# The last block's output products by seven block products, with weight sums formed on GpSimd and kept in DRAM

## The chip, the cores and the metric

One core of a Trainium2 chip runs the whole program. The metric is the device time of one execution in microseconds, as the median of the runs. The core has a matrix engine (PE, with weight loads shown apart as PEld), a vector engine (DVE), an activation engine (ACT), GpSimd (POOL), and a queue engine (SP) that issues the DMAs.

## The reference

Chunked attention with 8 memory keys gives `x` of 3072 tokens by 512. After it comes a two-layer network with a leaky bend; its second product is what the change touches:

```python
def _moe_ref(x, w_in, w_out, alpha):        # x 3072x512, w_in 512x2048, w_out 2048x512
    h = x @ w_in
    g = np.maximum(h, 0.0) + alpha * np.minimum(h, 0.0)
    return (g @ w_out).astype(np.float32)
```

## The kernel before

**Tiling.** The 3072 tokens are 8 half-blocks of `BT` = 384. The first two run plainly, each with 16 slices `f` of 128 hidden columns. The other six form three big blocks of 768 tokens, `big(0)`, `big(1)`, `big(2)`. Every fp32 operand is held as a high and a low part, and every product is three matmuls: high by low, low by high, high by high.

**A big block.** The up product (`x @ w_in`) is done for a pair of slices at a time, `pair(i)`, i = 0 to 7, in Strassen's way: seven block products for eight, 42 matmuls of 384 columns (L1194). DVE adds their PSUM results up (`add_in`, L1215), ACT and DVE make the bend (`bent`, L1084 and L1087), and `rooms` splits a bent slice into its two parts: a cast on ACT (L1100) and a subtraction on DVE (L1104), into one of four rooms used in turn. A pair leaves four bent tiles: `c11` and `c21` belong to the first 384 tokens (slices 2i and 2i+1), `c12` and `c22` to the second 384. The first two are split at once; the other two are kept (`kept_at`).

**The down product.** `chunk(which, f, tt)` multiplies one slice with 128 tokens against all 512 output columns: three matmuls of 512 columns (L1126), accumulated in a PSUM bank over all 16 slices. `whole(0, f)` for the slices of pair i-1 stands behind the products of pair i. After the last pair come the rest of `which` 0, and then `which` 1 with the slices in the order `later[s]`, each split by `take` just ahead of its use. `leave` copies the sums out of PSUM on ACT (L1259) and sends them.

**Weights.** They do not stay in SBUF. The up weights of a pair (`far_a`, `far_b`, with their Strassen sums) and the output weights of a pair (`far_o`) lie in DRAM and are loaded into slots 9 to 15, each with a queue of its own (`queues`, `load`), a slot's next load standing behind the last use of what it holds. The Strassen sums of the up weights are made by `sum_far(i, gate)`: on POOL two sums of the high and low part (L914), four sums and differences (L917) and two low parts (L925), on ACT two casts (L922), then two writes to DRAM by SP (L928). Pairs 0 to 4 are summed early; pairs 5, 6 and 7 late (`LATE_AT`), inside the big blocks.

**Order.** All work is first listed as steps with an engine, a cost and what they read and write. `Plan.send` sorts them by these costs into one fixed order for each engine, in which `rest` (a due time counted back from the end, with the constant `BIG`) decides between steps that could start. A write to DRAM is assumed to land 3.1 us after its issue (`LAND`), plus the step's `more`. On the chip each engine follows its order and waits where something is late.

**Attention inside the big blocks.** Blocks 0 and 1 still carry the attention of later units: `meet` puts value products and new scores on PE, and `weights` and `turn` put one POOL product (L415) and 21 transposes on DVE (L436) for each unit. `forms` subtracts and splits the next block's inputs (L989 on POOL; L971 on ACT; L975 on POOL and DVE). Block 2 carries no attention.

Of the kernel before, what the change touches and what calls it, by code (L numbers as in the profile page):

```python
# [70 lines left out]

HOP, LAND, FOLLOW = 0.07, 3.1, 0.1
# [15 lines left out]
PAIR, BIG = 4.7, 438.4  # L88
# [16 lines left out]
LATE_AT = {(0, 0): 5, (0, 5): 6, (1, 2): 7}  # L105
# [3 lines left out]
FIRST_SLOW = 28  # L109

# [84 lines left out]
def body(ctx: ExitStack, tc: tile.TileContext, qvw, kw, whole, heads, w_in, w_out, alpha, out):  # L195
# [53 lines left out]
    nc.scalar.activation(out=warm, in_=warm, func=AF.Exp)  # L249

# [599 lines left out]
    def store(blk, o_ps):  # L850
        def copy(tt, at_, o):
            if blk == 1:
                o["t"] = kept[tt]
                nc.vector.tensor_tensor(out=o["t"], in0=o_ps[tt], in1=o["t"], op=ALU.add)
            else:
                o["t"] = at_[0].tile([P, DM], F32, name="o_t", tag=at_[1])
                nc.scalar.copy(out=o["t"], in_=o_ps[tt])

        def send(tt, o):
            r = blk * BT + tt * P  # L860
            nc.sync.dma_start(out=out[r:r + P, :], in_=o["t"])

        for tt in range(NTT):
            at_ = (None, None, [("tmp", tt)]) if blk == 1 else leave_at(0)
            o = {}
            place = PLACE[blk, NF - 1] + 1
            step(DVE if blk == 1 else ACT, 0.68 if blk == 1 else 0.59, partial(copy, tt, at_, o), reads=okeys(blk),
                 writes=at_[2], rest=rest(place))
            step(SP, 0.75, partial(send, tt, o), reads=at_[2])
# [4 lines left out]
    far_r = {i: far.tile([P, 4 * HALF], F32, name=f"far_r{i}", tag=f"r{i}") for i in range(FIRST_LATE, NFP)}  # L874
    far_o = [far.tile([P, 2, 2, DM], F32, name=f"far_o{i}", tag=f"o{i}") for i in range(NFP)]
# [19 lines left out]
    def sum_far(i, gate):  # L895
        late = i >= FIRST_LATE
# [12 lines left out]
        def full(n):  # L909
            w = t[n] if late else ws[2 * i + n, 0].bitcast(F32)  # L910
# [18 lines left out]

        whole = [[("rs", n, 0), ("rs", n, 1)] + ([("f", n, 1)] if n or late else []) for n in range(2)]  # L930
# [4 lines left out]
        def raw_sum(n):  # L935
            step(POOL, 1.3, partial(full, n),
                 reads=gate + ([("f", n, 0)] if late else [("w", 0, 2 * i + n, 0), ("w", 0, 2 * i + n, 1)]), writes=whole[n])
# [4 lines left out]
        def form(n, to, key):  # L942
# [3 lines left out]
                 more=3.0 if late else 0.0)  # L946
            step(SP, 0.7, partial(put, n, to), reads=[("f", n, 0), ("f", n, 1)], writes=[key], more=FETCH / 2 if late else 0.0)

        a, b = far_a[i], far_b[i]
        raw_sum(0)  # L950
        raw_sum(1)
        add((1, 1), (1, 0), (1, 1), ALU.add)
# [64 lines left out]
    for b in range(NBIG):  # L1017
        for i in pairs_of[b]:
# [3 lines left out]
            queues[13 + i % 3].append(("o", b, 0, i))  # L1022
# [3 lines left out]
        for j, f in zip(order[NSTAY:], ([9, 10] if b == NBIG - 1 else []) + [11, 12] + stay):  # L1026
            queues[f].append(("o", b, 1, j))
    for f, q in queues.items():
        for x in q:
            home[x] = f  # L1030

    def load(f):
# [3 lines left out]
        x = queues[f].pop(0)  # L1036
        into = x[0] == "i"
# [22 lines left out]
    fresh = []  # L1060

    def big(s):
        ups, downs = UP[s % 2], UP[1 - s % 2]
        half = NPLAIN + 2 * s
        o = [{}, {}]
        pairs = pairs_of[s]
        turns = [list(BEFORE) if s == 0 else [], later[s]]
# [111 lines left out]

        def pair(i):  # L1180
# [47 lines left out]
            sk = bent(h, "c11", lambda: h[0], ("tmp", 0), f0)  # L1228
            rooms(g[0, f0], "c11", f0, lambda: h["c11"], sk)
# [8 lines left out]
            sk = bent(h, "c21", lambda: h[2], ("tmp", 2), f1)  # L1238
            rooms(g[0, f1], "c21", f1, lambda: h["c21"], sk)
# [3 lines left out]
            if i:  # L1243
                for f in (2 * i - 2, 2 * i - 1):
                    whole(0, f)
            if i:
                used(0, i - 1)
# [7 lines left out]
        def leave(which, tts, end=False):  # L1255
# [5 lines left out]
            def send(tt, x):  # L1261
                r = (half + which) * BT + tt * P
                nc.sync.dma_start(out=out[r:r + P, :], in_=x["t"])

            def send_half(tt, x, i):
                r, cols = (half + which) * BT + tt * P, slice(i * DM // 2, (i + 1) * DM // 2)
                (nc.scalar, nc.sync)[i].dma_start(out=out[r:r + P, cols], in_=x["t"][:, cols])

            for tt in tts:
                at_, x = leave_at(1 if s == 0 else 2), {}  # L1270
                step(ACT, 0.59, partial(copy, tt, at_, x), reads=[(downs, ups)[which][tt][2]], writes=at_[2],
                     rest=BIG - clock[0])
                if end and tt == NTT - 1:
                    for i in range(2):
                        step((ACT, SP)[i], 0.4, partial(send_half, tt, x, i), reads=at_[2])
                else:
                    step(SP, 0.75, partial(send, tt, x), reads=at_[2])
# [51 lines left out]
        for i in pairs:  # L1329
            if (s, i) in LATE_AT:  # L1330
                sum_far(LATE_AT[s, i], [("pair", s, i - 1)] if i else [("gate", len(ORDER) - 1)])
            think()
# [5 lines left out]
        last = s == NBIG - 1  # L1338
        if (s, NFP) in LATE_AT:
            sum_far(LATE_AT[s, NFP], [("pair", s, pairs[-1])])  # L1340
        rest_of = later[s]
# [8 lines left out]
        for n, f in enumerate(rest_of[:NF - NEND] if last else rest_of):  # L1350
            if n < 2:
                continue
            think()
            take(f)
# [5 lines left out]
        if not last:  # L1360
            leave(1, range(NTT))
            return
        for f in rest_of[NF - NEND:]:
            take(f)
        for tt in range(NTT):
            for f in rest_of[NF - NEND:]:
                chunk(1, f, tt)
            leave(1, [tt], end=True)
# [133 lines left out]
```

## Time and profile before

| | |
|---|---|
| three runs | 579.97, 580.73, 580.74 us, median 580.73 |
| span of the profiled execution | 578.6 us (first to last instruction) |
| PE, PEld busy | 569.9 us (98%), 505.1 us (87%) |
| DVE, ACT, POOL busy | 447.4 us (77%), 301.9 us (52%), 167.8 us (29%) |
| DMA | 154.68 MB, 267 GB/s over the span |
| big blocks 0, 1, 2 begin at about | 174, 316, 451 us |

The profiled execution has its own time: its span is 2.1 us under the median of the runs, which counts what lies around the span too. A PE row's busy time is modelled, since matmuls overlap; how fast matmuls follow each other is read from the chain of work, where each piece stands with its length and count.

### The profile page before, as it was taken

Reading aid. Unit: us, or ns where it says so; the run is one execution under the profiler, and the core shown is the slowest. Engines: PE = TensorE matmul, PEld = TensorE weight load, DVE = VectorE, ACT = ScalarE, POOL = GpSimd, SP = SyncE. Lnnn points to the kernel's source line nnn. Section 1 sums busy time; section 2 is a strip of 40 time slices with the busy share of each in tenths; the row PEclk is TensorE's granted clock in tenths of the full one; section 3 lists DMA queues with packets and bytes.
Section 4 is the critical chain, followed back from the end, with each engine's and each line's share of the span. In section 5 each row is a group of like instructions: output and inputs, shape, how many; then the busy total and the mean of one; then the engine's idle time right before and its main releaser. Section 6 shows DMA issues by size and latency. Waiting matters only on the chain.

```text
span 578.6 us, 11932 instructions
## 1 busy us (share of the span) xinstructions
PE 569.9 (98%) x4467; PEld 505.1 (87%) x4467; DVE 447.4 (77%) x995; ACT 301.9 (52%) x780; POOL 167.8 (29%) x190
## 2 busy tenths in 40 slices
PE   7999999999999999999999999999999999999997
PEld 4898989898989998999888998899888999999885
DVE  7989999888978999998989899876575566466420
ACT  3888888655665644536655453335434433223421
POOL 5640000046799935007416233003014300000000
PEclk9999999999999999999999999999999999999999
DMA  8999990386977779888797987784665867774601
GB/s 317 395 418 416 412 374 1 137 314 212 374 277 251 259 294 387 289 290 327 255 337 261 320 302 272 293 294 160 239 221 208 301 219 271 261 258 165 258 1 55
DMA packets 42090, 154.68 MB, mean 267 GB/s; under 512 B 4784, under 2 KB 10160, under 8 KB 34480
## 3 DMA queue, kind: packets, MB, share of 16 engines
q1 hardware_dynamic: 41888, 153.79, 72.5%
q8 instruction: 35, 0.57, 0.4%
q14 instruction: 23, 0.19, 0.1%
q10 hardware_dynamic: 144, 0.13, 0.1%
HBM read 122.97 MB, written 30.93 MB: 266 GB/s over the span
## 4 chain that ended last, share of the span: by engine, by line
PE 95%; DMA 2%; DVE 2%; ACT 0%; issue 0%; DVEq 0%
PE b_ps L1126 34%; PE b_ps L1194 28%; PE h_ps L774 12%; PE o_ps L804 12%; PE b_ps L1163 3%; PE a_ps L459 3%; PE s_ps L360 2%; DMA early<-heads 2%; PE a_ps L619 1%; PE o_ps L606 1%; DVE u L1215 1%; DVE pt L436 0%; PE s_ps L335 0%; DVE den L581 0%; DVE gl L1104 0%
## 5 line engine op out<-in xcount | busy, mean ns | idle before, releaser
L1194 PE MATMUL b_ps<-xf,wa 128*128 128x384 f32 x924 | 166.6, 336 | 0.3 <-ACT plain L533 0.2
L1194 PEld LDWEIGHTS b_ps<-xf,wa 128*128 128x128 f32 x924 | 160.9, 188 | 3.8 <-DVE u L1215 1.1
L1215 DVE TENSOR_TENSOR u<-b_ps,u 128x384 f32<-128x384 f32 x154 | 78.3, 551 | 47.3 <-PE b_ps L1194 41.8
L436 DVE STREAM_TRANSPOSE pt<-e 32x192 f32<-32x192 f32 (+1 forms) x336 | 100.0, 301 | 9.3 <-PE a_ps L459 2.1
L1084 ACT ACTIVATE g<-u 128x384 f32<-128x384 f32 x88 | 45.9, 525 | 77.8 <-DVE u L1215 69.2
L1126 PE MATMUL b_ps<-wo,xh 128*128 128x512 f32 x276 | 85.4, 391 | 0.0
L1126 PE MATMUL b_ps<-wo,gh 128*128 128x512 f32 x276 | 85.4, 391 | 0.0
L415 POOL TENSOR_TENSOR e<-e,den 128x384 f32<-128x384 f32 x24 | 20.9, 885 | 174.2 <-DVE den L409 77.4
L774 PE MATMUL h_ps<-xh,w 128*128 128x384 f32 x256 | 65.4, 336 | 0.0
L1126 PEld LDWEIGHTS b_ps<-wo,gh 128*128 128x128 f32 x276 | 51.8, 188 | 10.4
L1126 PEld LDWEIGHTS b_ps<-wo,xh 128*128 128x128 f32 x276 | 51.8, 188 | 10.4
L1126 PE MATMUL b_ps<-wo,gl 128*128 128x512 f32 x138 | 54.2, 393 | 0.0
L1126 PE MATMUL b_ps<-wo,xl 128*128 128x512 f32 x138 | 53.9, 391 | 0.0
L804 PE MATMUL o_ps<-w,xh 128*128 128x512 f32 x168 | 52.6, 394 | 0.0
L774 PEld LDWEIGHTS h_ps<-xh,w 128*128 128x128 f32 x256 | 46.4, 188 | 0.9
L394 ACT ACTIVATE e<-s_ps,mx 128x64 f32<-128x64 f32 x144 | 43.0, 327 | 4.1 <-DVE mx L386 4.1
L774 PE MATMUL h_ps<-xl,w 128*128 128x384 f32 x128 | 44.0, 344 | 0.0
L989 POOL TENSOR_TENSOR plain<-plain 128x384 f32<-128x384 f32 x24 | 26.3, 1116 | 44.2 <-ACT plain L533 43.0
L804 PEld LDWEIGHTS o_ps<-w,xh 128*128 128x128 f32 x168 | 31.5, 188 | 6.2
L804 PE MATMUL o_ps<-w,xl 128*128 128x512 f32 x84 | 33.0, 393 | 0.0
L394 ACT ACTIVATION_READ_ACCUMULATOR e<-s_ps,mx 128x1 f32 x144 | 31.7, 220 | 0.0
L1126 PEld LDWEIGHTS b_ps<-wo,gl 128*128 128x128 f32 x138 | 25.9, 188 | 5.5
(120 smaller groups left out, 889.2 us busy)
## 6 DMA issues: line engine op xcount, KB each, us to landing
wo<-far_o SPq DMA_DIRECT2D x37, 1024.0 KB, 6.3
wa<-far_a SPq DMA_DIRECT2D x22, 1024.0 KB, 7.3
wa<-far_b SPq DMA_DIRECT2D x22, 768.0 KB, 4.4
w_t<-w_in SPq DMA_DIRECT2D x16, 512.0 KB, 9.8
w_t<-w_out SPq DMA_DIRECT2D x16, 512.0 KB, 9.6
far_o<-w SPq DMA_DIRECT2D x16, 512.0 KB, 7.4
qk<-kw SPq DMA_DIRECT2D x24, 272.0 KB, 4.4
v_t<-qvw SPq DMA_DIRECT2D x24, 256.0 KB, 5.9
```

The costliest lines, as they stand in the source:

```text
L394: nc.scalar.activation(out=st["e"][:, i], in_=st["s"][h2][:, n], func=AF.Exp, scale=SCALE, bias=d["mx"][:, u - us[0], n, h2:h2 + 1], accum ...
L415: nc.gpsimd.tensor_tensor(out=st["e"], in0=st["e"], in1=st["den"].broadcast_to([P, NJ * 2, KW]), op=ALU.mult)
L436: nc.vector.transpose(out=pts[u % NPT][quad * CH:(quad + 1) * CH, j, t0:t0 + n1 - n0].rearrange("p t h q -> p (t h) q"), in_=(st["e"], zer ...
L459: nc.tensor.matmul(out=st["a"][h2 * D:(h2 + 1) * D, t * TQ:(t + 1) * TQ], lhsT=st["v"][:, t, h2, :], rhs=pts[u % NPT][:, :, t, h2, :], sta ...
L774: nc.tensor.matmul(out=h["ps"][:, :BT], lhsT=ws[f, 0][:, wk, k * P:(k + 1) * P], rhs=parts(blk, k)[1](xk), start=(k == 0 and n == 0), stop ...
L804: nc.tensor.matmul(out=o_ps[tt], lhsT=h[gk][:, tt * P:(tt + 1) * P], rhs=ws[f, 1][:, wk], start=(f == first_f and i == 0), stop=(f == last ...
L989: step(POOL, 1.15, lambda: nc.gpsimd.tensor_tensor(out=plain_at(to[0]), in0=plain_at(a[0]), in1=plain_at(b[0]), op=ALU.subtract), reads=[a ...
L1084: nc.scalar.activation(out=h[name], in_=src(), func=AF.Relu, scale=-1.0)
L1126: nc.tensor.matmul(out=o[which][tt], lhsT=h[gk][:, tt * P:(tt + 1) * P], rhs=w[:, wk].bitcast(F32R), start=(f == turns[which][0] and i == ...
L1163: nc.tensor.matmul(out=h["ps"], lhsT=ws[f, 0][:, wk, k * P:(k + 1) * P], rhs=xf[FORMS.index(names[k // 2])][:, xk, k % 2], start=(k == 0 a ...
L1194: nc.tensor.matmul(out=h[bank[1]][:, :BT], lhsT=weight(wk, p).bitcast(F32R), rhs=xf[xi][:, xk, p], start=p == 0 and k == 0, stop=p == 1 an ...
L1215: nc.vector.tensor_tensor(out=h[t], in0=h[bank[1]][:, :BT], in1=h[t if of is None else of], op=ALU.add)
```

## The change

Only block 2's down product changes, with what feeds it. The output is formed transposed, as 512 output columns by 768 tokens, and cut into two by two blocks: columns in halves of 256, the hidden size in even and odd slices, tokens in halves of 384. The seven products are A11 by c11, A12 by c21, S1 by T1, S2 by T2, S4 by c22, S3 by T3, and A22 by T4. Each is 8 slices by 2 column tiles by 3 matmuls of 384 columns.

- `form_down` makes T1 to T4 with four POOL subtractions for each pair. T1 and T4 take the place of c11 and c21, T3 that of c12; `extra` finds room for c11, c21 and T2 in tiles that the attention has left.
- `early_down(i-1)` does the A11 and A12 products behind pair i; `finish` does the last of these and the other five, with 40 more splits by `rooms`, the sums of the products on ACT and DVE, and the sending in the transposed layout.
- S1 to S4 are sums of output weights. `sum_far(i, gate, down)` makes them for pair i from the loaded output weights of block 0 or 1 (two L914, three L917, two L922, two L925) and SP writes four pieces of 256 KB to `far_s`. Pairs 6, 7 are done in block 0 after its pairs, 1 to 5 in block 1 at its pairs 2 to 6, and 0 after them. The late up sum of pair 7 moves from block 1's pair 2 to its pair 3.
- A11, A12, A22 and S1 to S4 are loaded by `load_down` (`LAST_ROOMS`), in place of block 2's output weights.
- Block 1's results leave over two staging tiles, not five. The host puts the transposed part back.

```diff
-PAIR, BIG = 4.7, 438.4
+PAIR, BIG = 4.7, 431.4
-LATE_AT = {(0, 0): 5, (0, 5): 6, (1, 2): 7}
+LATE_AT = {(0, 0): 5, (0, 5): 6, (1, 3): 7}
+DOWN_AT = {(1, 2): 1, (1, 3): 2, (1, 4): 3, (1, 5): 4, (1, 6): 5}
+DOWN_REST = {(0, 4): 6, (0, 6): 7, (1, 2): 0}
+LAST_ROOMS = ((13, "A1", 0), (14, "A1", 1), (15, "S1", 0), (13, "A1", 2), (14, "A1", 3), (13, "S1", 1), (9, "S2", 0),
+              (10, "S2", 1), (11, "S4", 0), (12, "S4", 1), (14, "S3", 0), (15, "S3", 1), (13, "A22", 0), (9, "A22", 1))
+LAST = (("S1", "T1"), ("S2", "T2"), ("S4", "c22"), ("S3", "T3"), ("A22", "T4"))
...
         raw_sum(0)
         raw_sum(1)
+        if down is not None:
+            add((1, 1), (0, 1), (1, 1), ALU.add)
+            add((0, 1), (0, 0), (0, 1), ALU.subtract)
+            add((0, 0), (1, 1), (0, 0), ALU.subtract)
+            form(0, ("S2", "S3"), None)
+            add((1, 0), (1, 0), (0, 0), ALU.subtract)
+            form(1, ("S4", "S1"), None)
+            return
...
+        def form_down(i):
+            place, keys = claim("T2", i)
+            for to, a, b in (("T1", "c12", "T1"), ("T3", "c22", "T3"), ("T2", "c22", "T1"), ("T4", "T4", "T2")):
+                ...
+                step(POOL, 1.15, less, reads=[ka, kb], writes=keys if to == "T2" else [kt])
...
+        def product_down(x, h, gk, i, bank, m, opened, closed):
+            ...
+            f = home[x, h]
+            pe(0.52, go, [("wa", f)] + [("wa", f, j) for j in range(4)] + [f"gh{n}", f"gl{n}"], [bank[2]])
...
+        def early_down(i):
+            for x in range(2):
+                ...
+                for m in range(2):
+                    product_down("A1", i // 2, ("A1", x, i), i, low_banks[2 * x + m], m, i == 0, i == NFP - 1)
+            if i % 2:
+                load(home["A1", i // 2])
...
             bent(h, "c12", lambda: h[1], ("tmp", 1), f0, *kept_at(f0))
-            if i:
+            if last:
+                form_down(i)
+                if i:
+                    early_down(i - 1)
+            elif i:
                 for f in (2 * i - 2, 2 * i - 1):
                     whole(0, f)
-            if i:
                 used(0, i - 1)
...
-                at_, x = leave_at(1 if s == 0 else 2), {}
+                at_, x = leave_at(1 if s == 0 else 0), {}
...
+            for n, (x, name) in enumerate(LAST):
+                for i in range(NFP):
+                    if n == 0 and i == 2:
+                        early_down(end)
+                        for m in range(2):
+                            copy("P1", m, low_banks[m])
+                        for m in range(2):
+                            add("C11", "P1", m, low_banks[2 + m], (0, 0, m))
+                    take_down(x, name, i)
+                    if x == "A22" and i >= NFP - NEND:
+                        continue
+                    for m in range(2):
+                        late_down(x, name, i, banks[x][m], m, i == 0, i == end)
+                    if i == 3 or i == end:
+                        load(home[x, i // 4])
+                for m in range(2):
+                    if x == "S2":
+                        add("u2", "P1", m, banks[x][m])
+                        add("P1", "u2", m, banks["S1"][m])
+                    ...
+                    elif x == "A22":
+                        for i in range(NFP - NEND, NFP):
+                            late_down(x, name, i, banks[x][m], m, False, i == end)
+                        add("u2", "u2", m, banks[x][m], (1, 0, m), 1 + m)
```

## Rows read from the trace of the kernel before

**Rows 1.** The page: busy time, its share of the span, instructions.
```profile
PE 569.9 (98%) x4467; PEld 505.1 (87%) x4467; DVE 447.4 (77%) x995; ACT 301.9 (52%) x780; POOL 167.8 (29%) x190
```
**Rows 2.** PE's waits from 330 us on: us in total, times, longest.
```profile
PE s_ps L360 <- issue: 0.7, 1, 0.7
```
**Rows 3.** Chain of waits: start us, length us, what.
```profile
360.91 1.47 PE a_ps L459 x32
...
398.92 7.34 PE b_ps L1194 x42
...
522.67 4.12 PE b_ps L1126 x18
526.80 7.30 PE b_ps L1194 x42
534.10 40.86 PE b_ps L1126 x180
574.98 0.58 ACT o_t L1259
```
**Rows 4.** Groups by line and form from 376 us: busy us, mean ns, idle before.
```profile
L1215 DVE TENSOR_TENSOR u<-b_ps,u 128x384 f32<-128x384 f32 x77 | 38.8, 551 | 41.0 <-PE b_ps L1194 37.6 <-ACT e L394 1.8 <-issue 1.0
L989 POOL TENSOR_TENSOR plain<-plain 128x384 f32<-128x384 f32 x8 | 8.9, 1134 | 35.2 <-ACT plain L533 35.2
L1104 DVE TENSOR_TENSOR gl<-g,gh 128x384 fp32r<-128x384 f32 x12 | 6.6, 552 | 0.2
L1100 ACT CAST gh<-g 128x384 fp32r<-128x384 f32 x12 | 6.2, 513 | 7.3 <-DVE g L1087 7.3
```
**Rows 5.** Windows: stretch and length us; busy (instructions) of PE, PEld, DVE, ACT, POOL; PEclk, DMA share, GB/s.
```profile
326.30:337.80 11.50, 11.50 (x63) 10.78 (x61) 10.03 (x24) 7.59 (x32) 0.00 (x0) 1.00 0.87 309
337.80:349.30 11.50, 11.50 (x61) 10.72 (x61) 10.46 (x22) 3.76 (x11) 6.19 (x6) 1.00 0.87 331
```
**Rows 6.** The same view, one pair of block 2.
```profile
515.37:526.80 11.43, 11.43 (x61) 10.69 (x61) 6.76 (x13) 3.62 (x7) 0.00 (x0) 1.00 0.71 262
```
**Rows 7.** DVE in order of time, around the end of a block 2 pair.
```profile
521.67 1.95 DVE L1215 TENSOR_TENSOR u<-b_ps,u 128x384 f32<-128x384 f32 x4 [0.70 <-PE b_ps L1194]
...
525.72 0.56 DVE L1104 TENSOR_TENSOR xl<-g,xh 128x384 fp32r<-128x384 f32 x1
```
**Rows 8.** The tile `form` of `sum_far`: ns min/median/max, first and last start.
```profile
L917 POOL TENSOR_TENSOR form<-form x17: 732/737/992, 118.6 to 348.1; 128x256 f32<-128x256 f32 x17
...
L925 POOL TENSOR_TENSOR form<-form x11: 1277/1292/1603, 132.6 to 353.0; 128x512 fp32r<-128x512 f32 x11
...
L914 POOL TENSOR_TENSOR form<-form x6: 1292/1298/1617, 206.5 to 343.9; 128x512 f32<-128x512 f32 x6
...
DMA to landing us min/median/max: 2.6/5.8/10.3
```
**Rows 9.** POOL in order of time: start us, length us.
```profile
317.98 1.99 POOL L975 TENSOR_TENSOR xf<-plain,xf 128x384 fp32r<-128x384 f32 x2
...
345.43 3.64 POOL L917 TENSOR_TENSOR form<-form 128x256 f32<-128x256 f32 x4
...
442.18 5.86 POOL L989 TENSOR_TENSOR plain<-plain 128x384 f32<-128x384 f32 x5 [16.03 <-ACT plain L533]
```
**Rows 10.** DVE in order of time beside those POOL rows.
```profile
346.90 0.55 DVE L1104 TENSOR_TENSOR xl<-g,xh 128x384 fp32r<-128x384 f32 x1
347.37 1.10 DVE L1087 SCALAR_TENSOR_TENSOR gs<-g,rise,u 128x384 f32<-128x384 f32 x1
348.39 1.09 DVE L1087 SCALAR_TENSOR_TENSOR g<-g,rise,u 128x384 f32<-128x384 f32 x1
349.40 0.60 DVE L1087 SCALAR_TENSOR_TENSOR gs<-g,rise,u 128x384 f32<-128x384 f32 x1
...
355.62 0.49 DVE L436 STREAM_TRANSPOSE pt<-e 32x64 f32<-32x64 f32 x2
...
442.62 2.29 DVE L975 TENSOR_TENSOR xf<-plain,xf 128x384 fp32r<-128x384 f32 x2 [0.78 <-ACT xf L971]
```
**Rows 11.** SP's issues in order of time, and landings of the up weights, 330 to 410 us.
```profile
382.36 0.32 SPq L1042 DMA_DIRECT2D wa<-far_b  x1
...
DMA to landing us min/median/max: 4.2/6.1/9.3
```

## What the change will do to the time, predicted blind

> **What bounds the kernel now.** First the busy shares: PE works 98% of the span [rows 1]. Since a busy PE need not be PE at its peak, the waits of PE come next: from 330 us on there is one of 0.7 us and no more [rows 2]. Then the chain of waits, which in block 2 is PE from end to end: a pair's products take 7.30 us for 42 matmuls, the output products behind them 4.12 us for 18, and after the last pair 180 matmuls of the down product follow each other in 40.86 us; one ACT copy of 0.58 us ends it [rows 3]. So matmul time taken out of block 2 comes off the end one for one, as long as whatever feeds PE keeps up. Feeding is loose in block 2 (DVE 6.76 us and POOL nothing in a pair of 11.43 us [rows 6]) and tight in block 1 (DVE 10.03 and 10.46 of 11.50 us, DMA share 0.87 [rows 5]). The change takes PE work from the loose place and puts POOL, SP and DMA work into the tight one as well. These two places are what has to be weighed.
>
> **Removed from PE.** Block 2's down product is 2 x 16 slices x 3 token tiles x 3 = 288 matmuls of 512 columns. Of these 180 take 40.86 us; the other 108 stand behind pairs 1 to 6 as six pieces of 4.12 us, 24.7 us [rows 3]. Together 65.6 us, or 228 ns each.
>
> **Added to PE.** Seven products x 8 slices x 2 column tiles x 3 = 336 matmuls of 384 columns with a new weight tile each. The pair products are the same form: 42 in 7.30 us, 173.8 ns each [rows 3], so 336 take 58.4 us. Net **-7.2 us**. An eighth less multiplication would be 8.2 us; the difference is the fixed part of each of 48 more matmuls.
>
> The Trainium skill (TensorE: Matmul & The Clock Gate, Back-to-back issue gap) states columns / 2.4 plus 2.5 ns for one matmul behind another; an estimate by it is 215.8 and 162.5 ns here. The trace differs, with 227 ns (40.86 / 180) and 173.8 ns. By that estimate 62.2 - 54.6 = 7.6 us would be saved and the time 0.4 us lower; the rows decide.
>
> **The pairs of block 2 get shorter.** Behind a pair now stand 12 matmuls of `early_down`, 2.1 us, in place of 18, so a pair lasts 9.4 us. DVE needs 6.76 us of it, no more than before, and POOL gets four subtractions of 1.13 us [rows 4, 6]: 4.5 us where it had nothing. Both fit. The next pair's first product needs a PSUM bank that DVE's four additions free; they end 0.95 us after the pair's last product (521.67 + 1.95 against 522.67 [rows 3, 7]), before the 2.1 us are over. Cost taken: 0; if POOL held up one DVE operation in each pair by a whole 1.13 us, DVE would still be at 7.9 of 9.4 us.
>
> **The entry to the closing stage.** Let E be the end of pair 7's products, and count from it. PE does 2.1 us of `early_down(6)`, then wants T1 of pair 0. Its split needs the room of c11 of pair 6, free after half of that, at 1.05. A cast of 0.51 and a subtraction of 0.55 us [rows 4] with a hand-over each make 2.3: PE stands 0.3 us. In that time DVE is also in its run at a pair's end, which lasts to 3.6 after E (525.72 + 0.56 against 522.67 [rows 3, 7]). If the split of T1 comes behind the whole run, it is ready at 4.2 and PE stands 2.1 us. The same happens on a smaller scale after `early_down(7)`, where T1 of pair 2 waits for a room until half of it is through: 0.2 us. POOL's four subtractions for pair 7 fall into the same 8 us and may hold a split up. From then on four rooms run ahead of PE by 3 x 1.04 us, and a split takes 1.2 us; DVE has 40 splits and some 15 additions of 0.55 us, 30 us in 42 us of PE time. I take **+0.9 us** for the entry, between 0.3 and 3, near the lower end since the order is by due time and T1 is due first.
>
> **The tail.** Before, an ACT copy of 0.58 us and a half transfer from each of two queues. After, DVE adds the last tile in two halves, each between 0.28 us (half of 0.55) and 0.55 [rows 4], and sends them from the same two queues: -0.3 to +0.5 us, I take 0.
>
> **The sums of output weights.** One `sum_far` of the new kind costs POOL 2 x 1.30 + 3 x 0.74 + 2 x 1.29 = 7.4 us [rows 8], eight of them 59 us, and SP 32 issues of 0.3 to 0.4 us. POOL was busy 167.8 of 578.6 us [rows 1] and has the room. Nothing waits for the sums themselves before the closing stage, 40 us and more later. What they can hold up is the work beside them.
>
> DVE first. An operation with both inputs in SBUF was slower beside POOL in some cases and not in others: L1104 took 0.55 us while POOL ran L917 (345.43 to 349.07), two L1087 in the same stretch 1.10 and 1.09 us, where 0.60 us is usual, and two L975 beside L989 2.29 us together, 0.6 us more each [rows 9, 10]. Pairs 2 and 3 of block 1 get 15 us of new POOL work in about 34 us before the next `meet`; there are 18 such DVE operations, 8 of them hit, at 0 to 0.6 us, so 0 to 4.8 us. The transposes that `meet` waits for end at 356.1 and its value products start at 360.91 [rows 3, 10]: 4.8 us of cover. Without that cover it would be up to 4.8 us on PE.
>
> Then SP and the DMAs. A load of up weights is issued at 382.36 and used by the pair at 398.92, 16.6 us later; the landing takes 6.1, at most 9.3 us [rows 3, 11]: 7.3 us of cover at the least. Four puts of 256 KB make 1.05 MB in a pair, 92 GB/s more; at 309 GB/s the share is 0.87, so it becomes 1.13, which is 1.5 us late for each such pair, and the five in a row could use up the cover.
>
> Output weights have three slots and more cover. Block 1's results over two staging tiles instead of five can make the third copy on ACT wait for a landing; the order foresees that wait. I take **+0.8 us** for all of this in blocks 0 and 1, between 0 and 3.5.
>
> **Sum.** 578.6 - 7.2 + 0.9 + 0.8 = 573.1 us span. With the 2.1 us between span and median, **575.2 us**. All terms at their kind ends: 573.3 or so; the forecast's own range is 573.9 to 576.6.
>
> **Rivals.**
>
> *1. The vector engine is blocked by POOL (the other side).* If every two-input DVE operation that meets a sum waits for a whole POOL instruction of 1.3 us, the 8 hits before `meet` in block 1 cost 10.4 us, 5.6 beyond the cover; the sums of pairs 6 and 7, 15 us of POOL in block 0's rest with attention on DVE too, cost about as much again, say 4.3. Then 575.2 + 9.9 = 585.1 us. It turns slower from about 1.0 us for each hit. For it: DVE at 10.46 of 11.50. Against: hits cost 0 to 0.6 us in rows 10. Beside it, the Trainium skill (SBUF — State Buffer, Who interferes with whom) says that a DVE instruction with two SBUF inputs and a GpSimd one that reads SBUF exclude each other for a whole instruction, whoever comes first. By that rule this case is real; the trace agrees in part, with 1.10 us for 0.60 and 0.55 for 0.55. Chance 0.10.
>
> *2. POOL and SP queues run late.* The order gives a put 3.1 us to land; landings of these tiles took 5.8 us, up to 10.3 [rows 8]. The next sum writes the same tile, so POOL stands 2.7 to 7.2 us, and what is queued behind it stands too: the next block's forms (POOL's last for block 1 end at 319.97, 4 us after the block has begun [rows 9]) and SP, which waits at the next put with weight loads behind it. With two late sums in a row, 5.4 to 14.4 us against 7.3 of cover: 0 to 7, about 3 us. Time 576.6 to 580, centred on 578. For it: pair 3 of block 1 carries two sums. Against: `more` = 3.0 puts slack before each put. Chance 0.22.
>
> *3. Everything is covered.* No loss in blocks 0 and 1, 0.3 us at the entry: 573.6 us or a little less. Chance 0.08, since 59 us of work beside tight engines seldom costs nothing.
>
> That the change does not do what it says is excluded for PE: 336 matmuls for 288 are counted in the code. A remaining 0.02 is for what I do not see.
>
> **The numbers.** The forecast has 0.58. A measurement of this kernel can tell 0.2% from no change, 1.2 us. Faster than 579.6: 0.58 + 0.08 + 0.18 of rival 2 + 0.02 of rival 1 = 0.86. Within: 0.03 + 0.03 + 0.01 = 0.07. Slower than 581.9: 0.01 + 0.05 + 0.01 = 0.07. The range reaches from the kind ends, 573.3, to 578.8, inside rival 2; outside lie rival 1, a third of rival 2, and the rest, not quite 2 in 10.
>
> **What would show it.** Right: 336 matmuls with 173.8 ns between them, PE's waits at the entry near 1 us, pairs of block 2 of 9.4 us, meets at the same times to 1 us, and block 2 starting at 451 to 452 us. Wrong: PE waiting for DVE in block 1's pairs 2 to 4 or at block 1's start (rival 1), PE waiting for `wa` landings or forms, with SP waiting for L925 (rival 2), or a wait in every pair of block 2, which would mean that the shorter pair is too short for its chain.

## The result and the profile after

The changed kernel takes 588.0 us (median of four executions, 586.4 to 591.2) against 580.7 us: a ratio of 1.013, 95% interval 1.009 to 1.017. It is 7.3 us slower; the prediction was 5.5 us faster. The profiled execution has a span of 589.4 us, the longest of the four.

The page of the kernel after, its row of busy times:

```profile
PE 570.3 (97%) x4515; PEld 512.3 (87%) x4515; DVE 493.4 (84%) x1034; ACT 319.1 (54%) x816; POOL 275.8 (47%) x286
```

Beside [rows 1], POOL has 108 us more (59 us of sums as worked out before, 33 us of `form_down` at 4.16 a pair, the rest longer instructions) and DVE 46 us more for 39 more instructions. The kernel without sums (below) has the same 1034 DVE instructions in 473.3 us, so 26 us are the new ones and 20 us are instructions that became longer.

The lines have moved: L1194 is now L1367 (the transposed products are L1321), L1126 is L1223, L1215 is L1388, L1087 is L1184, L1104 is L1201, L975 is L1007, L914, L917 and L925 are L930, L933 and L941. `put_down` writes at L947, the old loads are L1101, and S1 to S4 are loaded at L1081. PE's waits from 20 us on, us in total, times, longest:

```profile
PE b_ps L1367 <- DMA wa<-far_a: 3.7, 1, 3.7
PE b_ps L1367 <- DVE u L1388: 2.7, 3, 1.6
PE b_ps L1367 <- DVE xf L1007: 2.1, 1, 2.1
PE b_ps L1223 <- DVE xl L1201: 2.0, 1, 2.0
PE b_ps L1321 <- DVE gl L1201: 0.9, 1, 0.9
```

Where [rows 2] had one wait of 0.7 us, four of these five are new and outside the closing stage. The chain of waits says where:

```profile
299.77 9.32 DMA far_sS<-form
309.22 1.87 POOL form L930
...
317.62 1.09 DVE xf L1007
...
390.56 1.52 DVE gl L1201
392.09 1.57 DVE plain L1184
393.66 1.58 DVE g L1184
...
461.95 3.16 PE b_ps L1367 x18
...
481.95 10.18 DMA wa<-far_a
492.27 9.08 PE b_ps L1367 x42
...
503.43 7.28 PE b_ps L1367 x42
510.71 2.08 PE b_ps L1321 x12
...
546.97 39.30 PE b_ps L1321 x222
```

Three things are to be seen. Ahead of block 1 the chain runs along the landing of a write of sums: POOL's next sum waits for it, the next block's forms stand behind that sum in POOL's queue, and PE waits 2.1 us for a form (`xf`). In block 1 the chain leaves PE again and runs along DVE's two-input operations; the chain of [rows 3] had none of them in block 2 and PE in the pairs of block 1 that are shown. And at 481.95 it runs along one load of up weights. Block 1 began at 316 us, as before, and block 2 begins at 462 instead of 451: 11 us are lost in block 1 of this execution, the slowest of the four. From there to the end it takes 127.4 us, where it took 128.0, so block 2 gains only 0.6 us of the 6.3 forecast.

Windows of the same kernel (columns as in [rows 5]):

```profile
316.00:326.00 10.00, 7.85 (x124) 6.50 (x123) 7.35 (x17) 5.50 (x12) 10.00 (x11) 0.83 0.98 324
...
492.30:543.00 50.70, 50.70 (x284) 50.70 (x285) 34.64 (x66) 19.11 (x39) 18.55 (x18) 0.97 0.71 263
...
503.43:512.79 9.36, 9.36 (x55) 9.36 (x55) 6.81 (x14) 3.55 (x8) 4.16 (x4) 1.00 0.52 201
...
316.00:450.00 134.00, 127.24 (x871) 111.92 (x870) 114.87 (x232) 61.65 (x160) 79.33 (x74) 0.97 0.81 287
```

A pair of block 2 lasts 9.36 us, as forecast, with DVE at 6.81. But the column of the granted clock, 1.00 throughout in [rows 5] and [rows 6], is below 1 here: PE, after waits of 2.1, 2.0 and 3.7 us, ran at 1.2 GHz for some 3.4 us each time (a mean of 0.83 over the first 10 us is 3.4 us at half). That is part of the 9.08 us for 42 matmuls behind the wait, 1.8 more than the 7.28 of the later pairs.

The DVE part of the chain, in order of time:

```profile
388.61 1.95 DVE L1388 TENSOR_TENSOR u<-b_ps,u 128x384 f32<-128x384 f32 x4
390.48 1.61 DVE L1201 TENSOR_TENSOR gl<-g,gh 128x384 fp32r<-128x384 f32 x1
392.01 1.65 DVE L1184 SCALAR_TENSOR_TENSOR plain<-g,rise,u 128x384 f32<-128x384 f32 x1
393.58 1.64 DVE L1184 SCALAR_TENSOR_TENSOR g<-g,rise,u 128x384 f32<-128x384 f32 x1
395.15 0.61 DVE L1184 SCALAR_TENSOR_TENSOR plain<-g,rise,u 128x384 f32<-128x384 f32 x1
```

and POOL in the same stretch:

```profile
390.38 1.30 POOL L941 TENSOR_TENSOR form<-sum,form 128x512 fp32r<-128x512 f32 x1 [2.48 <-ACT form L938]
391.63 1.62 POOL L941 TENSOR_TENSOR form<-form 128x512 fp32r<-128x512 f32 x1
393.20 1.61 POOL L930 TENSOR_TENSOR sum<-wo 128x512 f32<-128x512 f32 x1
```

Three DVE operations behind each other follow POOL's rhythm, one for each POOL instruction, at 1.61 to 1.65 us where [rows 4, 10] have 0.55 and 0.60. The fourth, with POOL idle again, takes 0.61. POOL's own instructions go from 1.3 to 1.6 us. The four additions of L1388 just before, which have one input in PSUM, take 1.95 us as in [rows 7], but POOL stood idle beside nearly all of them. Their mean over block 1 shows that they are not hit: 552 ns here, in this row, and 552 in the same stretch of the kernel before.

```profile
L1388 DVE TENSOR_TENSOR u<-b_ps,u 128x384 f32<-128x384 f32 x56 | 28.7, 552 | 4.8 <-ACT u L1380 1.5 <-issue 1.4 <-PE b_ps L1367 1.2
```

The other half is in SP's queue. SP and POOL waits of the kernel after, 300 to 540 us and 260 to 460 us, then the landings of the new writes and SP's issues in order of time:

```profile
SPq L1101 <- POOL form L930: 18.2, 4, 6.2
...
SPq L1081 <- DMA far_sS<-form: 7.4, 1, 7.4
```

```profile
POOL form L930 <- DMA far_sS<-form: 27.8, 5, 8.9
```

```profile
DMA to landing us min/median/max: 2.1/6.5/9.4
```

```profile
469.83 0.33 SPq L1101 DMA_DIRECT2D wa<-far_a  x1
470.25 1.00 SPq L947 DMA_DIRECT2D far_sS<-form  x1
478.69 0.32 SPq L1081 DMA_DIRECT2D ws<-far_sS  x1
479.11 2.05 SPq L947 DMA_DIRECT2D far_sS<-form  x3
...
481.95 0.47 SPq L1101 DMA_DIRECT2D wa<-far_a  x1
```

The first row is SP at the loads of weights, into slots that a sum still reads. Then SP issues the write of pair 0's S1 at 470.25 and wants to load S1 right behind it, so it stands for the landing until 478.69. The up weights of the pair at 488 us stand behind it, are issued at 481.95, take 10.18 us, and PE waits 3.7 us. S1 itself is first used at 540.7, some 60 us after its load is issued.

### The profile page after: what moved, and what is told of

Same layout as the page of the kernel before. It is cut to its first block, busy times and chain, and to the rows that moved or that the text cites. A ratio compares the mean times of both kernels' runs of the same rounds, so it can differ in the third digit from the quotient of the medians.

```text
span 589.4 us, 12368 instructions
## 1 busy us (share of the span) xinstructions
PE 570.3 (97%) x4515; PEld 512.3 (87%) x4515; DVE 493.4 (84%) x1034; ACT 319.1 (54%) x816; POOL 275.8 (47%) x286
## 4 chain that ended last, share of the span: by engine, by line
PE 81%; DVE 9%; DMA 4%; POOL 2%; issue 1%; ACT 1%; SPq 1%; DVEq 0%; POOLq 0%
PE b_ps L1367 22%; PE b_ps L1223 16%; PE h_ps L788 12%; PE o_ps L818 11%; PE b_ps L1321 9%; PE b_ps L1260 3%; PE a_ps L473 2%; PE s_ps L374 2%; DVE u L1388 2%; DVE pt L450 2%; DMA wa<-far_a 2%; DMA far_sS<-form 2%; DVE gl L1201 1%; PE a_ps L633 1%; DVE g L1184 1%
## 5 line engine op out<-in xcount | busy, mean ns | idle before, releaser
L1367 PE MATMUL b_ps<-xf,wa 128*128 128x384 f32 x924 | 170.1, 340 | 8.9 <-DMA wa<-far_a 3.7
L1367 PEld LDWEIGHTS b_ps<-xf,wa 128*128 128x128 f32 x924 | 162.5, 190 | 14.1 <-DVE u L1388 4.6
L1388 DVE TENSOR_TENSOR u<-b_ps,u 128x384 f32<-128x384 f32 x154 | 78.7, 552 | 31.7 <-issue 17.1
L429 POOL TENSOR_TENSOR e<-e,den 128x384 f32<-128x384 f32 x24 | 22.5, 948 | 137.2 <-ACT e L408 74.0
L1223 PE MATMUL b_ps<-wo,xh 128*128 128x512 f32 x180 | 57.0, 399 | 0.0
L1223 PE MATMUL b_ps<-wo,gh 128*128 128x512 f32 x180 | 55.7, 391 | 0.0
L1223 PEld LDWEIGHTS b_ps<-wo,xh 128*128 128x128 f32 x180 | 34.5, 192 | 6.9
L1223 PEld LDWEIGHTS b_ps<-wo,gh 128*128 128x128 f32 x180 | 33.8, 188 | 6.8
L1223 PE MATMUL b_ps<-wo,xl 128*128 128x512 f32 x90 | 36.1, 401 | 2.0 <-DVE xl L1201 2.0
L1223 PE MATMUL b_ps<-wo,gl 128*128 128x512 f32 x90 | 35.6, 395 | 0.0
L941 POOL TENSOR_TENSOR form<-form 128x512 fp32r<-128x512 f32 x19 | 26.1, 1377 | 9.7 <-ACT form L938 9.7
```

Of the source, the lines that this page charges most:

```text
L429: nc.gpsimd.tensor_tensor(out=st["e"], in0=st["e"], in1=st["den"].broadcast_to([P, NJ * 2, KW]), op=ALU.mult)
L941: nc.gpsimd.tensor_tensor(out=t[n][:, 1].bitcast(F32R), in0=r[n], in1=t[n][:, 0].bitcast(F32), op=ALU.subtract)
L1223: nc.tensor.matmul(out=o[which][tt], lhsT=h[gk][:, tt * P:(tt + 1) * P], rhs=w[:, wk].bitcast(F32R), start=(f == turns[which][0] and i == ...
L1367: nc.tensor.matmul(out=h[bank[1]][:, :BT], lhsT=weight(wk, p).bitcast(F32R), rhs=xf[xi][:, xk, p], start=p == 0 and k == 0, stop=p == 1 an ...
L1388: nc.vector.tensor_tensor(out=h[t], in0=h[bank[1]][:, :BT], in1=h[t if of is None else of], op=ALU.add)
```

## The experiments

The sums of S1 to S4 have three parts that can be taken away singly: POOL's instructions, the writes, and where the loads stand in SP's queue.

**No sums and no writes.** `DOWN_AT` and `DOWN_REST` are empty and S1 to S4 are loaded from `far_o`, so the products use other weights than the sums.

```diff
-DOWN_AT = {(1, 2): 1, (1, 3): 2, (1, 4): 3, (1, 5): 4, (1, 6): 5}
-DOWN_REST = {(0, 4): 6, (0, 6): 7, (1, 2): 0}
+DOWN_AT = {}
+DOWN_REST = {}
```

> Left out: the sums of output weights (POOL, ACT and their writes); S1 to S4 are loaded with the same bytes from far_o instead, so block 2 runs its seven products with the same instructions on other weights. Theory A (POOL's sums slow DVE operations with two SBUF inputs, DVE then holds PE up in blocks 0 and 1): the PE saving comes out, 574 to 576 us. Theory B (landings of the sums' writes hold POOL and SP up, forms and up weights come late): the same, 574 to 576 us. If the loss lies in block 2 itself (shorter pairs, form_down beside DVE, the closing stage), it stays above 580 us.

573.6 us, ratio 0.988 (0.987 to 0.990). PE has one wait after 20 us:

```profile
PE b_ps L1321 <- DVE gl L1201: 0.9, 1, 0.9
```

So block 2's part of the forecast holds, the entry's 0.9 us included, and all 14.4 us up to 588.0 come from sums and writes.

**Sums without writes.** S1 to S4 are loaded from `far_o` here too.

```diff
-            for k2, x in enumerate(to):
-                step(SP, 0.7, partial(put_down, n, k2, x), ...)
```

> Left out: only the writes of the sums to DRAM; POOL and ACT form all eight sums as in the change, S1 to S4 are loaded from far_o. POOL no longer waits for a landing and SP for no sum. Theory A: the loss stays, 583 us or more, with PE waiting for DVE in block 1. Theory B: 575 to 578 us, no halving of the granted clock after long idle times of PE.

583.7 us, 1.005 (1.003 to 1.007): +10.1 for the sums alone.

**Writes without sums.** The 32 pieces are written from the loaded output weights (other values than the sums), and POOL and ACT do nothing for them.

```diff
+                nc.sync.dma_start(out=far_s[x, i // 4][:, i % 4], in_=wa[down][:, n, :, k2 * HALF:(k2 + 1) * HALF])
...
-        raw_sum(0)
-        raw_sum(1)
```

> Left out: the sums on POOL and ACT; SP writes the same 32 pieces of 256 KB to far_s, but straight from the loaded output weights, and S1 to S4 are loaded from far_s. DMA bytes and SP issues are those of the change, POOL's work is not there. Theory A: 574 to 577 us. Theory B, if it is the write traffic itself that makes up weights late: 580 us or more with PE waiting for wa; if it is POOL's standing that matters, 575 to 578 us.

578.7 us, 0.997 (0.995 to 0.998), so +5.1, between the expected ranges. But the whole loss is at one place in block 0's rest, where a write has to wait for the weights that it copies, and the score loads of attention stand behind it:

```profile
SPq L975 <- DMA wo<-far_o: 5.5, 1, 5.5
```

```profile
PE s_ps L374 <- ACT e L433: 3.2, 1, 3.2
```

Block 1 begins 5.4 us later than without writes. From 300 to 530 us PE doesn't wait: 1.05 MB more in a pair costs nothing in block 1. The prediction's arithmetic of DMA shares (0.87 to 1.13, 1.5 us late in a pair) falls.

**The order told of late landings.**

```diff
-step(SP, 0.7, partial(put_down, n, k2, x), ...)
+step(SP, 0.7, partial(put_down, n, k2, x), ..., more=FETCH / 2)
```

> The whole change, with one number of the order altered: the writes of the sums are taken to land 7.1 us after issue (3.1 before), so that POOL's and SP's orders put what depends on them later. Theory A: about 586 to 588 us, as the change. Theory B: most of the loss from standing POOL and SP goes, 577 to 582 us.

595.6 us, 1.027 (1.025 to 1.030), worse than either theory had it. PE waits 6.5 us for `wo` and 3.0 for `wa`, and SP stands longer at loads whose slot a sum still reads (27.7 us between 260 and 500 us, where the change has 18.2): the sums read their output weights later, and the slot is reloaded later.

**Fills in place of sums**, still without writes: POOL fills the same tiles (three fills for an instruction, of about the same time), so it writes SBUF and reads nothing. The rest of the order stays; the tiles don't hold sums.

```diff
-nc.gpsimd.tensor_tensor(out=part(*to), in0=part(*a), in1=part(*b), op=op)
+for _ in range(3):
+    nc.gpsimd.memset(part(*to), 0.25)
```

> The kernel without the writes of the sums (e2), with POOL's sums replaced by fills of the same tiles that take about as long (three memsets for each sum or difference), in the same order; S1 to S4 come from far_o. Left out: the sums and their writes. POOL is occupied as in e2 but reads no SBUF. Theory A1 (a DVE operation with two SBUF inputs and a POOL operation that reads SBUF hold each other up): the loss goes, 573.5 to 576 us. Theory A2 (POOL's in-order queue is what holds the forms and the attention's products up): the loss stays as in e2, 582 to 585 us.

576.6 us, 0.993 (0.992 to 0.995), just above the first case: 7.2 of the 10.1 us are gone. The plain bends of DVE between 316 and 450 us, first with sums (no writes), then with fills (busy us, mean ns):

```profile
L1182 DVE SCALAR_TENSOR_TENSOR plain<-g,rise,u 128x384 f32<-128x384 f32 x8 | 9.7, 1206 | 0.0
```

```profile
L1194 DVE SCALAR_TENSOR_TENSOR plain<-g,rise,u 128x384 f32<-128x384 f32 x8 | 4.9, 611 | 0.0
```

The kernel before has 611 ns in the same row. What DVE suffers from is POOL's reading, not POOL's work. The Trainium skill (SBUF — State Buffer, Who interferes with whom) says that a DVE instruction with two SBUF inputs contends with a GpSimd one that reads SBUF, and not with one that only writes it. Both halves agree: 1206 ns beside sums, 611 beside fills.

Not all of the loss goes that way. PE still waits 2.5 us here for two splits: ACT stands 2.0 us at the cast of a sum (L946) until POOL has filled it, and the casts of the splits stand behind that in ACT's queue. So POOL's occupation alone costs something too, over ACT.

**Other places.** The sums of pairs 0, 1, 2 go into block 1's rest, 3 to 5 into its pairs 4 to 6, and the late up sum of pair 7 back to pair 2; first without writes, then whole.

```diff
+DOWN_AT = {(1, 4): 3, (1, 5): 4, (1, 6): 5}
+DOWN_REST = {(0, 4): 6, (0, 6): 7, (1, 4): 0, (1, 6): 1, (1, 8): 2}
```

> As e2 (sums without their writes, S1 to S4 from far_o), with the sums of pairs 1 and 2 and 0 moved from block 1's pairs 2 and 3 and the start of its rest into its rest, where DVE is loose, and the late up sum of pair 7 back at pair 2. Theory A1 with a price that depends on how tight DVE is: 577 to 581 us, less than e2. If the price is the same everywhere: 583 to 585 us.

> The whole change with the placement of e6. Theory A1 plus a cost of the landings: 3 to 6 us over e6. If the landings' cost came from pairs 2 and 3 alone: within 2 us of e6.

581.0 us (1.001, 1.000 to 1.002) without writes, 2.7 less than in the old places; whole, 591.8 us (1.019, 1.017 to 1.022). Here the writes add 10.7 us, more than either expectation, so it isn't their number that costs. In the first of the two ACT stands 6.0 us at the cast of a sum (L938) for POOL, a copy of block 1's results (L1431) stands behind it, and PE waits 2.6 us for such copies; the whole one has 3.4 us of that wait, and no kernel with the old places has any.

**The writes from ACT's queue.**

```diff
-nc.sync.dma_start(out=far_s[x, i // 4][:, i % 4], ...)
+nc.scalar.dma_start(out=far_s[x, i // 4][:, i % 4], ...)
...
-step(SP, 0.7, partial(put_down, n, k2, x), ...)
+step(ACT, 0.4, partial(put_down, n, k2, x), ..., more=3.1)
```

> The whole change with its own placement, only the 32 writes of the sums are issued by ACT's queue and not by SP's. Theory B1 (SP stands at a write or at the load of S1 and holds weight loads up, and the writes land late behind 1 MB loads in the same queue): 583.5 to 585.5 us, near e2. Theory B2 (the landing takes as long from any queue and POOL waits for it): 587 to 589 us, as the change.

587.7 us, 1.011 (1.007 to 1.014), no change beyond the spread (585.1 to 590.3). The landing is 2.1/5.3/9.7 us and POOL waits 27.5 us for it, so the queue that issues isn't what makes them late. SP still stands 9.4 us at the load of S1; PE no longer waits for `wa`, but 2.4 us for `wo` and 2.5 for forms from POOL.

**Writes that no sum waits for.** The sums are made, but what is written comes from a constant tile, so the values are not the sums. Each write goes as two of half the size, so SP issues 64 in place of 32.

```diff
-nc.sync.dma_start(out=far_s[x, i // 4][:, i % 4], in_=t[n].bitcast(F32)[:, :, k2 * HALF:(k2 + 1) * HALF])
+for l in range(2):
+    nc.sync.dma_start(out=far_s[x, i // 4][:, i % 4, l], in_=busy.bitcast(F32))
```

> The change with its sums, its order and its 32 writes (same bytes, same steps), but what is written comes from a tile that nothing ever rewrites, so no sum on POOL waits for a landing; the values written are not the sums. Two theories for the 4.3 us between e2_sums_no_puts (583.72) and the change (588.0). Landing theory: they come from POOL's waits at L930 for far_sS landings (27.8 us, 5 times), so the time is that of e2, 583 to 585 us, and POOL shows no wait for far_sS. Traffic theory: they come from the writes in SP's queue and on the DMA engines; then 587 to 589 us with POOL waits gone all the same.

588.6 us, 1.013 (1.010 to 1.015). POOL no longer waits for a landing of sums, and the time is no less: that these waits make up the whole 4.3 us falls, unless the 32 more issues cost as much. PE's wait for a form at block 1's start shrinks from 2.1 to 0.6 us, but it waits 1.5 us for `wo` and 3.6 for `u` (none and 2.7 in the change). What stays is

```profile
PE b_ps L1368 <- DMA wa<-far_a: 3.6, 1, 3.6
```

```profile
SPq L1082 <- DMA far_sS<-busy: 7.2, 1, 7.2
```

which is the load of S1 behind the write that it reads.

**Early sums.** From output weights that still stand in SBUF: pairs 0 to 3, or 0 to 2, where POOL had nothing to do; pair 4, or pairs 3 and 4, late in block 1's rest. The first of the two gives other values than it should and counts for its time alone. The places of the second:

```diff
+DOWN_AT = {(1, 6): 5}
+DOWN_EARLY = {16: 0, 19: 1, 22: 2}
+DOWN_REST = {(0, 4): 6, (0, 6): 7, (1, 11): 3, (1, 13): 4}
...
+        if PLACE[blk, f] in DOWN_EARLY:
+            sum_far(DOWN_EARLY[PLACE[blk, f]], [("gate", PLACE[blk, f] - 1)], 1)
```

> The whole change, but the sums of pairs 0 to 3 are made at 85 to 125 us from the output weights that still stand in SBUF, where POOL is idle; 6 and 7 stay in block 0's rest, 5 at block 1's pair 6, 4 late in block 1's rest. The up sum of pair 7 goes back to pair 2. Port theory: most of block 1's loss of 11 us is gone, but in the early stretch DVE is 93% busy (18.6 of 20 us) and its two-input operations on SBUF (1.22, 1.22 and 0.56 us of each 6.5) are hit by 30 us of POOL work; against 5 us of slack there this costs 0 to 8 us, so 576 to 583 us, and a PE wait for DVE between 80 and 130 us if it is over 577. Landing theory (the loss is mostly POOL and SP standing for landings, DMA share there only 0.3): 574 to 576 us and no PE wait before 130 us.

> As e10_early, but only pairs 0 to 2 early and further apart (gates 16, 19, 22), pairs 3 and 4 in the last part of block 1's rest (slices 11 and 13). Port theory: fewer hits in the tight early stretch, 22 us of POOL work over 35 us; 575 to 580 us, at or below e10 unless the two late sums hit the forms of block 2 (then a PE wait at 440 to 465 us). Landing theory: same as e10 to 1 us, 574 to 576.

605.1 us (1.041, 1.039 to 1.043) and 599.1 us (1.031, 1.028 to 1.034), far outside both expectations. Both engines suffer. With three sums early, DVE and POOL:

```profile
99.81 1.80 DVE L716 SCALAR_TENSOR_TENSOR a<-a,w_t 128x1024 int32<-128x1024 int32 x1
101.53 2.43 DVE L708 COPY w_t<-w_t 128x1024 int16<-128x1024 int16 x1
103.77 1.58 DVE L813 TENSOR_TENSOR xl<-g,xh 128x384 fp32r<-128x384 f32 x1
```

```profile
100.49 2.27 POOL L944 TENSOR_TENSOR form<-sum,form 128x512 fp32r<-128x512 f32 x1
102.84 2.09 POOL L933 TENSOR_TENSOR sum<-w 128x512 f32<-128x512 f32 x1
```

The copy, which has one input, took at most 1.34 us in the change's own trace, and the low part 1.3 us on POOL: the idle POOL of that stage was no free resource. With three sums early, PE waits 3.1 us between 80 and 130 us and another 8.9 us between 130 and 316, behind the early sums, and block 1's pairs begin 18 us late. So the port theory had the sign and not the size; the larger part of the loss, outside the early stretch, was not traced.

**One load moved.** In the order, a load by SP behind a write by SP gets no landing time at all, since both are SP steps. Only for pair 0 it now gets 20 us. This changes one thing in the order of all engines: S1's first load stands behind four loads of up weights and two of output weights.

```diff
-                    wait = FOLLOW if engine == DVE else 0.0
+                    wait = FOLLOW if engine == DVE else more if more > FETCH else 0.0
...
-step(SP, 0.7, partial(put_down, n, k2, x), ...)
+step(SP, 0.7, partial(put_down, n, k2, x), ..., more=20.0 if i == 0 else 0.0)
```

> The whole change with one load moved in SP's queue: the load of S1's first half, which stood directly behind the write of pair 0's sum (SP stood there for its landing from 470.25 to 478.69 us, with the up weights of the coming pairs behind it), is issued after four loads of up weights and two of output weights, 10 us later in the queue and still 40 us before its use. The order of every other engine and of every other SP step is unchanged. Theory A (what the writes add to e2_sums_no_puts is this one stand of SP): the wait of 3.7 us for wa at 488 us and the half clock behind it, 1.7 us, are gone, so 588.0 - 5.4 = 582.6 us, 582 to 584, and what is left above e1_no_sums (573.6) is the reading of SBUF by POOL. Theory B (the writes cost by their traffic or by POOL's landing waits in block 1): 586 to 588 us, block 2 starting at 462 us as in the change and the wait for wa only moved.

582.3 us, 1.004 (1.002 to 1.005): 5.7 us for one load's place, as theory A said (2.7 to 8.2 by the ends of the two intervals). In the profile the wait for `wa` is gone, SP doesn't stand for a landing, and POOL waits for landings as before:

```profile
483.24 2.08 SPq L1077 DMA_DIRECT2D ws<-far_o  x2
485.38 0.61 SPq L1081 DMA_DIRECT2D ws<-far_sS  x1
```

```profile
POOL form L930 <- DMA far_sS<-form: 26.3, 5, 9.6
```

The profiled execution, the fastest of six, begins block 2 at 456.4 us, where the change's, the slowest of four, had 462.0. The moved load can't be the reason, since it comes later and every engine has the same order up to there: what block 1 loses differs by some 5 us from execution to execution. Read from block 2's begin, where the load matters, the rest takes 122.2 us in place of 127.4, so 5.2 us are the load's. The kernel without sums and writes takes 121.8.

**What is left.** The load moved as above, and fills in place of the sums, with the edit of `e5_fills` (the written values aren't the sums).

> e12_last_landing with POOL's sums of output weights replaced by fills of the same tiles, of about the same time and at the same places (written, not read); ACT's casts, the 32 writes and all loads stay, and what is written is not the sums. If POOL's reading beside DVE is what is left, and writes and landings are free: 576 to 578 us, as e5_fills (576.55). If writes still cost: 579 to 582.

580.5 us, 0.999 (0.998 to 1.001), in its second case: writes still cost. Rows of 316 to 450 us, from the kernel with the load moved and from this one (third pair of columns: DVE):

```profile
316.00:450.00 134.00, 128.95 (x915) 113.53 (x915) 118.87 (x236) 63.26 (x164) 81.86 (x76) 1.00 0.83 293
```

```profile
316.00:450.00 134.00, 129.61 (x922) 114.83 (x921) 102.61 (x238) 65.16 (x168) 82.78 (x175) 1.00 0.81 292
```

Reading makes DVE 16.3 us busier for about the same number of instructions, yet here it costs only 1.8 us at the end, where it cost 7.2 without writes. And the writes, with fills, cost 4.0 us (2.6 of them one wait for `wo` at 417 us). The two losses aren't additive: what is late for one cause covers what is late for the other.

**Two more placements**, with the load moved: the one of `e7_moved` (`more` for pairs 0 to 2), and one with pair 1's sum alone moved into the rest (`more` for pairs 0 and 1), which is shown; in both the up sum of pair 7 goes back to pair 2:

```diff
-DOWN_AT = {(1, 2): 1, (1, 3): 2, (1, 4): 3, (1, 5): 4, (1, 6): 5}
-DOWN_REST = {(0, 4): 6, (0, 6): 7, (1, 2): 0}
+DOWN_AT = {(1, 3): 2, (1, 4): 3, (1, 5): 4, (1, 6): 5}
+DOWN_REST = {(0, 4): 6, (0, 6): 7, (1, 2): 0, (1, 8): 1}
```

> The placement of e7_moved (sums of pairs 0 to 2 in block 1's rest, 3 to 5 in its pairs), whole change, with the landing of their writes foreseen in SP's queue, so that S1's load stands last. In the order the sum of pair 2 then falls into block 2. If e7's loss over e6_moved_no_puts (591.75 against 581.03) was SP's stand alone: 580 to 583 us. If sums beside the forms of block 2 cost by themselves: 584 to 592, with PE waiting for u or forms at 440 to 470 us.

> e12_last_landing with only the sum of pair 1 moved, from block 1's pair 2 into its rest (slice 8), and the up sum of pair 7 back at pair 2. By the port theory pairs 2 and 3, the tightest before a meet, are relieved: 580 to 582 us against 582.3; if the sum in the rest costs as much there, 582 to 586.

598.4 us (1.030, 1.029 to 1.032) and 588.8 us (1.017, 1.014 to 1.019), both above all that was expected. In the first PE waits 5.7 us for S1 itself, which is now too late, 6.6 us for `u` and 3.5 for a copy of block 1's results; in the second 4.4 for `u` and 1.6 for such a copy. So these places cost more than block 1's pairs, whatever the load does. No version with sums beat the kernel before.

## Why the prediction was wrong

**Right.** The matmul term and the pairs: net -7.2 + 0.9 us was forecast, and without sums and writes the kernel is 6.8 us under the one before (573.6 against 580.4, run on the same chip). Pairs of block 2 of 9.4 us (9.36) came as forecast, and the sum leaves nothing for the tail. The 0.9 us of the closing stage agree in size, and there luck has a part: PE doesn't stand at T1 of pair 0, where the text put 0.3 us, but 7.3 us after the pairs' end, behind `early_down(7)`, where it put 0.2; the split there took 1.23 us on DVE beside one of POOL's subtractions.

**The step that failed** is the sums of output weights: "+0.8 us for all of this in blocks 0 and 1, between 0 and 3.5". It measured 14.4 us (588.0 - 573.6), and 5 of them lie in block 2, where the text put nothing. Three parts of it were off.

*The price and the number of hits.* The text took 0 to 0.6 us for a hit, from rows where POOL did a few instructions, eight hits, and 4.8 us of cover ahead of a `meet`. Beside back-to-back sums a hit operation lasts as long as the POOL instruction beside it, 1.0 us more (1.61 to 1.65 for 0.55 to 0.60). The sums spread over all of block 1, and PE waited where the cover wasn't: with sums and no writes 4.0 us for the additions (`u`) and 3.9 us for splits. With sums alone that is 7.2 us (583.7 against 576.6 with fills). This is rival 1's mechanism, given 0.10 at 585.1 us. The row of 1.10 us for 0.60 in [rows 10] was already this effect, beside L917's instruction of 0.74 us; 0.55 for 0.55 was no counterexample: there DVE's operation had begun first (346.90), and the L917 that began beside it (347.07) took 0.98 us.

*The landing ahead of block 1.* Rival 2 put a landing late in front of the next sum's tile and of the next block's forms, and 3 us on it. That chain is there: POOL stands 27.8 us in all, and at block 1's start PE waits 2.1 us for a form and then runs at 1.2 GHz for 3.4 us. What it is worth by itself isn't shown: without the landing waits this wait is 0.6 us, but others are longer and the time is the same (588.6).

*SP's queue in block 2.* A load of S1 stood behind its own write's landing, in front of up weights: 5.2 to 5.7 us, 3.7 of them PE's wait and most of the rest its lower clock behind it. The text costed 32 issues and the landing of puts and never asked what is queued behind the load that reads them.

**What stays open.** With S1's load moved, 8.7 us remain (582.3 - 573.6), nearly all of them ahead of block 2 in its profile. They are shared by POOL's reading and the writes, and the shares depend on the order of removal (1.8 to 7.2 and -1.4 to 4.0 us). The 3.0 us between fills without writes (576.6) and no sums at all (573.6) go in part over ACT's queue (2.5 us of PE's waits in that profile), which the text never costed; no run takes that alone away. Sums in the rest of block 1 cost more once they are written, and no single wait accounts for it.

## What to carry to other kernels

Price a POOL instruction that reads SBUF at up to its whole length on every DVE operation with two SBUF inputs that it can meet (1.0 us for 1.3 here; additions that read PSUM weren't hit, one wide copy was); an idle POOL beside a DVE with no slack isn't free. Look also at what stands behind ACT's part of such a sum in ACT's queue. For each new write to DRAM look up which load reads it and what stands behind that load in the same queue: the load stands for the landing, however late its data is needed. Then remove sums, writes and queue places one at a time, and don't expect the losses to add up.

## What the hardware showed that was not expected

PE's clock fell in the middle of the kernel. In the profiled execution after, PE ran at 1.2 GHz for 3.4 us behind each of three idle stretches of 2.0 to 3.7 us, and not behind three shorter ones of 0.8 to 1.6. With the one load moved it idled 2.0 us at 412 us and kept its 2.4 GHz, and with fills and writes 2.6 us at 417 us, likewise. The mean clock also differs between executions of one kernel: with fills and writes, six of twelve have 0.997 and spans of 579.3 us in the mean, the other six, the profiled one among them, 0.999 to 1.0 and 577.7. That the same wait makes the difference is likely and not shown, since one execution of each kernel has a trace. A wait of some 2 us can thus cost nearly twice its length, or not. The kernel before has no such wait.

Writes of 256 KB landed 6.5 us after their issue in the median (2.1 to 9.4) from SP's queue and 5.3 (2.1 to 9.7) from ACT's, hardly sooner than the loads of 1 MB (medians of 6.3 to 7.6 by kind).
